# Second layer of an attention and mixture kernel: the polynomial evaluated from PSUM, and the next block's input prepared at other places of the step

## The chip, the cores and the metric

The kernel runs on one core of one Trainium2 chip. A core has five engines that run side by side, each through a queue of its own in program order: TensorE (PE, matrix products into PSUM; its weight loads are listed as PEld), VectorE (DVE), ScalarE (ACT), GpSimd (POOL) and SyncE (SP), which issues the transfers between HBM and SBUF. They wait for each other through semaphores only. The metric is the device time of one execution in microseconds (us).

## The reference

Eight sequences of 576 tokens with eight heads of 64 go through linear attention; the 4608 x 512 result goes through a gated layer (512 to 1536 to 512) and then through the second layer, with which this case is concerned:

```python
def _moe2_ref(x, w_in, w_out, a, b):          # x 4608 x 512, w_in 512 x 2048, w_out 2048 x 512
    h = x @ w_in
    h2 = h * h
    h3 = h2 * h
    P = a[0] + a[1] * h + a[2] * h2 + a[3] * h3
    Q = 1.0 + np.abs(b[0]) * np.abs(h) + np.abs(b[1]) * h2
    g = P / (Q + 1e-06)
    return g @ w_out
...
    x = ...attention of q, k, v...
    x = _moe_ref(x=x, **moe_kwargs)
    return _moe2_ref(x=x, **moe2_kwargs)
```

## The kernel before

All products are made in a reduced 32-bit format of TensorE. To keep the reference's precision every operand x is split into a high part (`th`, `gh`, `wh`: ScalarE copies x into the reduced format) and a low part (`tl`, `gl`: x minus the high part), and a product is three matmuls, high x high, high x low and low x high (`mm3`, L191 to L194). The split of `g` takes its low part on GpSimd (`split`, L183 and L185); that of the second layer's input takes it on VectorE (L1044 and L1046).

The second layer runs from about 966 us to 1787 us of the span. Its 4608 tokens are cut into nine blocks j of 512, the 2048 inner columns into eight groups m of 256: 72 steps i = 8j + m. `h` of a step is a product of 256 rows by 512 columns, built with seven half-size products in the manner of Strassen instead of eight (`product2`, six matmuls of 256 columns each). They accumulate in two PSUM tiles, `px` and `py`, of which there are two pairs, so that a step and the one before it each have one. Between the products, parts of `py` are copied out and added back: ScalarE copies into `s12` and `s5` (L1225, L1230, L1233), VectorE adds `py` (L1236, after product 4) and `px` (L1239, after product 5). Product 6 goes on top of the half of `py` that L1236 has read, so TensorE can begin it only then.

After product n of step i, `close(n)` issues the rest of the work at that place. Each engine's order is the order of issue. `close` calls:

- `vec(i, n)`: the operations on the step before, or on this one, as the table `VEC` lists them for n, each with its lag (1: the step before). For one step they are: ScalarE's square into `r` (L1098), absolute value into `ah` (L1102), and a2 h + a1 into `pp` (L1094), each from PSUM; VectorE's `ah` += b1 r (L1110) and `pp` += a3 r (L1106), which together with a multiplication of `pp` by h in PSUM (L1114, twice, one for `px` and one for `py`) gives P without a0; ScalarE's logarithm of Q into `r` (L1118) and exponential of its negative (L1122), that is 1/Q; two operations of VectorE that refine it (`u1` L1126, `u2` L1130); and `g` = (`pp` + a0) `ah` (L1134). `ah`, `pp` and `r` are tiles of 128 x 1024 in SBUF with two buffers each. `vec_split` splits `g` for the second product.
- the preparation of the next block's input, a generator `building` (`tb_all`): three times a step from m = 1 to 6 one of its pieces is issued, a high part, a low part, or one of GpSimd's four differences `tr` (L1053, L1057, L1060, L1063). The input itself comes into `x_raw`, which has one buffer, by a transfer of 1 MiB issued at the start of step m = 0 (L1202).
- `back_some`: 24 matmuls a step of 512 columns that multiply `g` of three steps earlier by the output weights and sum into four PSUM tiles `accb` (`back_b`, L1150). At a block's end VectorE and ScalarE copy `accb` out (L1156, L1158).
- `pull2`: the transfers of `wi`, the weights of one product, eight products ahead, all from SyncE's queue (L1076).

The tables and the two calls around which the change turns are these:

```python
    VEC = (
        ((vec_g, 2), (on(1, vec_id), 1)), ((on(1, vec_sq), 1), (on(1, vec_abs), 1), (vec_ah, 1), (on(0, vec_split), 2)),
        ((vec_pp, 1), (on(1, vec_split), 2)), ((vec_ln, 1), (on(0, vec_p2), 1)),
        ((vec_exp, 1), ), ((on(1, vec_p2), 1), (vec_u1, 1), (on(0, vec_id), 0)),
        ((vec_u2, 1), (on(0, vec_sq), 0), (on(0, vec_abs), 0)))
...
            if 1 <= m < NM - 1 and n in (1, 3, 5):
                next(building, None)
```

Of the kernel before, what the change touches and what calls it, by code (L numbers as in the profile page):

```python
# [26 lines left out]
HB = NB // 2  # L27
# [109 lines left out]
def kernel(ctx: ExitStack, tc: tile.TileContext, q, k, v, w1, w2, ab_in, out):  # L137
# [16 lines left out]
    def f32(ap):  # L154
        return ap.bitcast(F32)
# [280 lines left out]
    def wfree(n):  # L436
        live[0] -= n
# [596 lines left out]
    def quarter(k, t):  # L1034
        return x_raw[:, 2 * k:2 * k + 2, t * HB:(t + 1) * HB]

    def tb_split(j, n, src, eng):
        if j % 2 == 0 and n > 2:
            h, lo = x_h[:, n - 3, :], x_l[:, n - 3, :]
        else:  # L1040
            h, lo = wnew(F32R, "th"), wnew(F32R, "tl")
        h, lo = (x.rearrange("p (c t) -> p c t", t=HB) for x in (h, lo))
        TB[j, n] = h, lo
        nc.scalar.activation(h, src, AF.Copy)  # L1044
        yield
        eng.tensor_tensor(out=lo, in0=src, in1=f32(h), op=ALU.subtract)  # L1046
        yield

    def tb_all(j):
        b11, b12, b21, b22 = (quarter(k, t) for k in range(2) for t in range(2))  # L1050
        t = wnew(F32, "tr").rearrange("p (c t) -> p c t", t=HB)
        yield from tb_split(j, 0, b11, nc.vector)
        nc.gpsimd.tensor_tensor(out=t, in0=b12, in1=b11, op=ALU.subtract)  # L1053
        yield
        yield from tb_split(j, 1, b21, nc.vector)
        yield from tb_split(j, 3, t, nc.vector)
        nc.gpsimd.tensor_tensor(out=t, in0=b22, in1=t, op=ALU.subtract)  # L1057
        yield
        yield from tb_split(j, 5, b22, nc.vector)
        nc.gpsimd.tensor_tensor(out=b12, in0=b22, in1=b12, op=ALU.subtract)  # L1060
        yield
        yield from tb_split(j, 2, t, nc.vector)
        nc.gpsimd.tensor_tensor(out=t, in0=b21, in1=t, op=ALU.subtract)  # L1063
        yield
        yield from tb_split(j, 4, b12, nc.vector)
        yield from tb_split(j, 6, t, nc.vector)
        wfree(1)

    seq2 = [(i, n) for i in range(NBLK * NM) for n in range(NPROD)]
    ahead2 = [0]  # L1070
# [20 lines left out]

    def vec_id(i, k):
        ps, ah, pp, r = vb[i]
        nc.scalar.activation(pp[:, k], ps[k], AF.Identity, scale=ab[:, 2:3], bias=ab[:, 1:2])  # L1094

    def vec_sq(i, k):
        ps, ah, pp, r = vb[i]
# [3 lines left out]
        ps, ah, pp, r = vb[i]  # L1101
        nc.scalar.activation(ah[:, k], ps[k], AF.Abs, scale=babs[:, 0:1])  # L1102

    def vec_pp(i):
        ps, ah, pp, r = vb[i]
        nc.vector.scalar_tensor_tensor(out=pp, in0=r, scalar=ab[:, 3:4], in1=pp, op0=ALU.mult, op1=ALU.add)  # L1106

    def vec_ah(i):
        ps, ah, pp, r = vb[i]
# [1 line left out]

    def vec_p2(i, k):
        ps, ah, pp, r = vb[i]
        nc.vector.tensor_tensor(out=pp[:, k], in0=pp[:, k], in1=ps[k], op=ALU.mult)  # L1114

    def vec_ln(i):
        ps, ah, pp, r = vb[i]
# [50 lines left out]
    def on(k, fn):  # L1168
        return partial(fn, k=k)

    VEC = (
        ((vec_g, 2), (on(1, vec_id), 1)), ((on(1, vec_sq), 1), (on(1, vec_abs), 1), (vec_ah, 1), (on(0, vec_split), 2)),
        ((vec_pp, 1), (on(1, vec_split), 2)), ((vec_ln, 1), (on(0, vec_p2), 1)),
        ((vec_exp, 1), ), ((on(1, vec_p2), 1), (vec_u1, 1), (on(0, vec_id), 0)),
        ((vec_u2, 1), (on(0, vec_sq), 0), (on(0, vec_abs), 0)))

    def vec(i, n):
        for fn, lag in VEC[n]:
# [19 lines left out]

    for i in range(NBLK * NM):
        j, m = divmod(i, NM)  # L1200
        if m == 0 and j + 1 < NBLK:
            nc.sync.dma_start(out=x_raw, in_=x3_d[j + 1].rearrange("m p c -> p m c"))  # L1202
            building = tb_all(j + 1)
        if i > 2:
            backs += [back_b(i - 3, k) for k in range(2)]
        share = BACK_SHARE if i > 2 else (5, ) * 7
        ps = [ps_w.tile([P, NB], F32, tag=n, name=n) for n in ("px", "py")]
        vec_new(i, ps)
        xl, xr, yl, yr = (x[:, t * HB:(t + 1) * HB] for x in ps for t in range(2))
        s12 = tb.tile([P, NB], F32, tag="s12", name="s12")  # L1210
        s5 = tb.tile([P, HB], F32, tag="s5", name="s5")

        def close(n):
            vec(i, n)
            if 1 <= m < NM - 1 and n in (1, 3, 5):
                next(building, None)
            if m == NM - 2 and n == 6:
                run(building)
            back_some(share[n])
            if n in (1, 3, 5):  # L1220
                fetch_some()
            pull2(i * NPROD + n + 1 + AHEAD)

        product2(i, 0, yl)
        nc.scalar.activation(s12[:, :HB], yl, AF.Copy)  # L1225
        close(0)
        product2(i, 1, xl)
        close(1)
        product2(i, 2, yl)
        nc.scalar.activation(s12[:, HB:], yl, AF.Copy)  # L1230
        close(2)
        product2(i, 3, xr)
        nc.scalar.activation(s5, xr, AF.Copy)  # L1233
        close(3)
        product2(i, 4, yl)
        nc.vector.tensor_tensor(out=yr, in0=yl, in1=s5, op=ALU.add)  # L1236
        close(4)
        product2(i, 5, xr)
        nc.vector.tensor_tensor(out=ps[0], in0=ps[0], in1=s12, op=ALU.add)  # L1239
        close(5)  # L1240
        product2(i, 6, yl)
        close(6)
        if i == 2:
            back_all()
        if m == NM - 1:
            wfree(14 if j % 2 else 6)
# [48 lines left out]
```

## Time and profile before

| what | value |
| --- | --- |
| median of three runs | 1795.63 us (1794.71 to 1796.7) |
| the profiled execution | 1794.12 us, of which the span 1792.0 |
| mean granted clock of TensorE | 0.991 of 2.4 GHz |
| TensorE, matmuls | 1715.8 us busy, 96% of the span |
| TensorE, weight loads | 1444.8 us, 81% |
| VectorE | 1470.3 us, 82% |
| ScalarE | 1130.3 us, 63% |
| GpSimd | 604.5 us, 34% |
| DMA | 348.01 MB, 194 GB/s over the span |

The profiled execution's own time is the span plus what lies around it (2.1 us). Busy shares are of the whole span, in which the attention, the first layer and the second layer follow each other with different loads; what a change to the second layer is worth has to be read within that layer, step by step. The matmuls' ends are modelled, so TensorE's busy time is not a proof that it runs at its peak; where it waits, the row of the waiting matmul says for how long and for whom.

### The profile page before, as it was taken

The numbers are of one execution on the slowest core, as the hardware profiler recorded it, in microseconds if no ns is written. First come the engines' busy times: TensorE is split into PE (matmuls) and PEld (weight loads), VectorE is DVE, ScalarE is ACT, GpSimd is POOL, SyncE is SP. The second block draws the span as 40 slices with busy tenths as digits, with TensorE's granted clock in tenths as the row PEclk, the third lists the DMA queues.
The fourth block names the chain that finished last, engine by engine and source line by source line (L and its number), as shares of the span: only waits on it lengthen the run. The fifth ranks groups of instructions, "written<-read, shape, count | busy, mean of one in ns | idle before, by whom it ended". The sixth has DMA issues, their size and how long they took to land.

```text
span 1792.0 us, 27297 instructions
## 1 busy us (share of the span) xinstructions
PE 1715.8 (96%) x9480; PEld 1444.8 (81%) x9480; DVE 1470.3 (82%) x1914; ACT 1130.3 (63%) x1897; POOL 604.5 (34%) x380
## 2 busy tenths in 40 slices
PE   5989999999999999999999999999999999999998
PEld 4767877888778887788887888888888888888897
DVE  8998897646665657677775899999999999999997
ACT  4565446555664466544444677777777777777775
POOL 2013342211223312252225434343434344434433
PEclk8999999999999999999999999999999999999999
DMA  6551775235674556548986875655565556555550
GB/s 212 175 179 65 246 247 178 63 117 187 224 245 136 199 187 215 194 141 277 329 298 233 310 238 172 230 172 192 172 223 176 189 177 217 171 190 185 184 200 24
DMA packets 193128, 348.01 MB, mean 194 GB/s; under 512 B 18912, under 2 KB 54752, under 8 KB 192992
## 3 DMA queue, kind: packets, MB, share of 16 engines
q1 hardware_dynamic: 192992, 346.27, 57.6%
q8 instruction: 76, 1.25, 0.3%
q14 instruction: 60, 0.49, 0.1%
HBM read 282.23 MB, written 63.96 MB: 193 GB/s over the span
## 4 chain that ended last, share of the span: by engine, by line
PE 63%; DVE 17%; ACT 9%; issue 6%; DMA 3%; POOL 1%; SPq 0%; ACTq 0%; DVEq 0%; POOLq 0%
PE accb L1150 13%; PE acc L477 13%; DVE pp L1106 3%; PE pa L192 3%; PE pa L193 3%; PE pa L194 3%; PE py L192 3%; PE py L193 2%; PE py L194 2%; DMA wi<-wi 2%; PE px L193 2%; PE px L194 2%; PE px L192 2%; DVE tl L1046 2%; ACT pp L1094 2%
## 5 line engine op out<-in xcount | busy, mean ns | idle before, releaser
L185 POOL TENSOR_TENSOR gl<-pp,gh 128x512 fp32r<-128x512 f32 x144 | 275.7, 1935 | 456.0 <-ACT gh L183 299.8
L1150 PE MATMUL accb<-wh,gh 128*128 128x512 f32 x576 | 185.3, 394 | 2.5 <-ACT gh L183 2.2
L1150 PE MATMUL accb<-wl,gh 128*128 128x512 f32 x576 | 185.6, 395 | 0.0
L1150 PE MATMUL accb<-wh,gl 128*128 128x512 f32 x576 | 185.0, 394 | 0.0
L1118 ACT ACTIVATE r<-ah,ln_bias 128x1024 f32<-128x1024 f32 x72 | 82.9, 1151 | 156.3 <-DVE pp L1106 156.3
L1106 DVE SCALAR_TENSOR_TENSOR pp<-r,ab,pp 128x1024 f32<-128x1024 f32 x72 | 165.5, 2299 | 0.0
L192 PE MATMUL py<-th,wi 128*128 128x256 f32 x416 | 118.3, 284 | 14.8 <-DVE py L1236 13.5
L185 POOL TENSOR_TENSOR gl<-ga,gh 128x512 fp32r<-128x512 f32 x36 | 51.3, 1425 | 226.2 <-ACT gh L183 226.0
L194 PE MATMUL py<-tl,wi 128*128 128x256 f32 x416 | 117.3, 282 | 0.0
L193 PE MATMUL py<-th,wi 128*128 128x256 f32 x416 | 117.1, 281 | 0.0
L1150 PEld LDWEIGHTS accb<-wh,gl 128*128 128x128 f32 x576 | 100.2, 189 | 13.4
L1150 PEld LDWEIGHTS accb<-wh,gh 128*128 128x128 f32 x576 | 100.4, 189 | 13.1 <-ACT gh L183 2.7
L1150 PEld LDWEIGHTS accb<-wl,gh 128*128 128x128 f32 x576 | 100.5, 189 | 10.1
L1110 DVE SCALAR_TENSOR_TENSOR ah<-r,babs,ah 128x1024 f32<-128x1024 f32 x72 | 92.5, 1284 | 19.2 <-ACT ah L1102 18.6
L192 PEld LDWEIGHTS py<-th,wi 128*128 128x128 f32 x416 | 78.5, 189 | 30.5 <-DVE py L1236 20.1
L183 ACT ACTIVATE gh<-pp 128x512 fp32r<-128x512 f32 x144 | 92.6, 644 | 13.4 <-DVE pp L1134 12.2
L1126 DVE SCALAR_TENSOR_TENSOR ah<-ah,r 128x1024 f32<-128x1024 f32 x72 | 88.0, 1222 | 12.9 <-ACT r L1122 12.7
L185 POOL TENSOR_TENSOR hl<-val,hl 128x512 fp32r<-128x512 f32 (+1 forms) x32 | 38.2, 1194 | 171.0 <-ACT hl L183 84.2
L1134 DVE SCALAR_TENSOR_TENSOR pp<-pp,ab,ah 128x1024 f32<-128x1024 f32 x72 | 92.4, 1283 | 2.3
L1130 DVE SCALAR_TENSOR_TENSOR ah<-ah,r 128x1024 f32<-128x1024 f32 x72 | 89.0, 1236 | 1.9
L477 PE MATMUL acc<-gh,wh 128*128 128x512 f32 x288 | 88.6, 402 | 0.0
L477 PE MATMUL acc<-gl,wh 128*128 128x512 f32 x288 | 86.1, 394 | 0.4 <-POOL gl L185 0.4
(235 smaller groups left out, 5405.4 us busy)
## 6 DMA issues: line engine op xcount, KB each, us to landing
wi<-wi SPq DMA_DIRECT2D x504, 256.0 KB, 4.7
ws<-ws SPq DMA_DIRECT2D x252, 256.0 KB, 5.0
raw<-in_w SPq DMA_DIRECT2D x68, 512.0 KB, 4.8
v<-in_v SPq DMA_DIRECT2D x30, 325.0 KB, 4.1
k<-in_k SPq DMA_DIRECT2D x30, 320.0 KB, 3.7
q<-in_q SPq DMA_DIRECT2D x36, 256.0 KB, 3.7
x_raw<-x SPq DMA_DIRECT2D x9, 1024.0 KB, 7.7
out<-ob SPq DMA_DIRECT2D x36, 256.0 KB, 2.5
```

Source lines behind the costliest of these rows:

```text
L183: nc.scalar.activation(h, src, AF.Copy)
L185: lo_eng.tensor_tensor(out=lo, in0=src, in1=f32(h), op=ALU.subtract)
L192: nc.tensor.matmul(ps, wh, xh, start=first, stop=False, **kw)
L193: nc.tensor.matmul(ps, wl, xh, start=False, stop=False, **kw)
L194: nc.tensor.matmul(ps, wh, xl, start=False, stop=last, **kw)
L477: nc.tensor.matmul(accs["a", j][m], x[:, m * P:(m + 1) * P], y, start=(f == 0 and n == 0), stop=(f == NF1 - 1 and n == 2))
L1106: nc.vector.scalar_tensor_tensor(out=pp, in0=r, scalar=ab[:, 3:4], in1=pp, op0=ALU.mult, op1=ALU.add)
L1110: nc.vector.scalar_tensor_tensor(out=ah, in0=r, scalar=babs[:, 1:2], in1=ah, op0=ALU.mult, op1=ALU.add)
L1126: nc.vector.scalar_tensor_tensor(out=ah, in0=ah, scalar=q_one, in1=r, op0=ALU.add, op1=ALU.mult)
L1130: nc.vector.scalar_tensor_tensor(out=ah, in0=ah, scalar=2.0, in1=r, op0=ALU.subtract, op1=ALU.mult)
L1134: nc.vector.scalar_tensor_tensor(out=pp, in0=pp, scalar=ab[:, 0:1], in1=ah, op0=ALU.add, op1=ALU.mult)
L1150: nc.tensor.matmul(accs["b", j][t], x[:, t * P:(t + 1) * P], y, start=(f == 0 and n == 0), stop=(f == NF2 - 1 and n == 2))
```

## The change

The polynomial is evaluated in Horner's form. ScalarE's operation from PSUM now makes a3 h + a2 (L1096). `vec_pp`, the VectorE operation on 128 x 1024 with two inputs in SBUF, is gone. In its place the two multiplications by h in PSUM come first (`vec_p1`, L1108, a plain product), and two new operations follow (`vec_p2`, L1116): `pp` = (`pp` + a1) h, with a1 a column of one scalar for each partition, `pp` in SBUF and h in PSUM. VectorE thus has one operation more in a step.

The table `VEC` is written anew. Both of ScalarE's copies into `pp` and VectorE's `ah` and `g` follow product 0; the logarithm and the first multiplication product 1; both splits of `g` and the second multiplication product 2; the exponential and both new operations product 3; `u1` and `u2` stay behind products 5 and 6, and the squares and absolute values of both halves are taken in the same step.

The generator is gone. Of the next block's input, each step from m = 1 issues one high part and at most one of GpSimd's differences after product 4, and from m = 2 one low part right behind `g`, after product 0. The seventh low part of a block is issued in the block's own step m = 0. The transfer into `x_raw` stands behind it, in `close(0)` of step m = 0, and reads or writes nothing else than before. TensorE's instructions keep their order.

```diff
-    def tb_split(j, n, src, eng):
+    def tb_hi(j, n):
...
+    def tb_lo(j, n):
+        h, lo = TB[j, n]
+        nc.vector.tensor_tensor(out=lo, in0=tb_src.pop(n), in1=f32(h), op=ALU.subtract)
...
+    def tb_add(j, n):
+        b11, b12, b21, b22 = (quarter(k, t) for k in range(2) for t in range(2))
+        if n == 3:
+            tb_src["t"] = wnew(F32, "tr").rearrange("p (c t) -> p c t", t=HB)
+        t = tb_src["t"]
+        out, x, y = {3: (t, b12, b11), 2: (t, b22, t), 4: (b12, b22, b12), 6: (t, b21, t)}[n]
+        nc.gpsimd.tensor_tensor(out=out, in0=x, in1=y, op=ALU.subtract)
...
-        nc.scalar.activation(pp[:, k], ps[k], AF.Identity, scale=ab[:, 2:3], bias=ab[:, 1:2])
+        nc.scalar.activation(pp[:, k], ps[k], AF.Identity, scale=ab[:, 3:4], bias=ab[:, 2:3])
...
-    def vec_pp(i):
+    def vec_p1(i, k):
         ps, ah, pp, r = vb[i]
-        nc.vector.scalar_tensor_tensor(out=pp, in0=r, scalar=ab[:, 3:4], in1=pp, op0=ALU.mult, op1=ALU.add)
+        nc.vector.tensor_tensor(out=pp[:, k], in0=pp[:, k], in1=ps[k], op=ALU.mult)
...
     def vec_p2(i, k):
         ps, ah, pp, r = vb[i]
-        nc.vector.tensor_tensor(out=pp[:, k], in0=pp[:, k], in1=ps[k], op=ALU.mult)
+        nc.vector.scalar_tensor_tensor(
+            out=pp[:, k], in0=pp[:, k], scalar=ab[:, 1:2], in1=ps[k], op0=ALU.add, op1=ALU.mult)
...
     VEC = (
-        ((vec_g, 2), (on(1, vec_id), 1)), ((on(1, vec_sq), 1), (on(1, vec_abs), 1), (vec_ah, 1), (on(0, vec_split), 2)),
-        ((vec_pp, 1), (on(1, vec_split), 2)), ((vec_ln, 1), (on(0, vec_p2), 1)),
-        ((vec_exp, 1), ), ((on(1, vec_p2), 1), (vec_u1, 1), (on(0, vec_id), 0)),
-        ((vec_u2, 1), (on(0, vec_sq), 0), (on(0, vec_abs), 0)))
+        ((on(0, vec_id), 1), (on(1, vec_id), 1), (vec_ah, 1), (vec_g, 2)),
+        ((vec_ln, 1), (on(0, vec_p1), 1)),
+        ((on(0, vec_split), 2), (on(1, vec_split), 2), (on(1, vec_p1), 1)),
+        ((vec_exp, 1), (on(0, vec_p2), 1), (on(1, vec_p2), 1)),
+        (),
+        ((vec_u1, 1), (on(0, vec_sq), 0), (on(0, vec_abs), 0)),
+        ((vec_u2, 1), (on(1, vec_sq), 0), (on(1, vec_abs), 0)))
+    TB_LO = (4, None, 0, 3, 1, 2, 5, 6)
+    TB_HI = (None, 0, 3, 1, 2, 5, 6, 4)
+    TB_ADD = (None, 3, 4, 2, None, 6, None, None)
...
-            if 1 <= m < NM - 1 and n in (1, 3, 5):
-                next(building, None)
-            if m == NM - 2 and n == 6:
-                run(building)
+            if n == 0:
+                if m == 0 and 0 < j:
+                    tb_lo(j, 4)
+                if m == 0 and j + 1 < NBLK:
+                    nc.sync.dma_start(out=x_raw, in_=x3_d[j + 1].rearrange("m p c -> p m c"))
+                if 1 < m and j + 1 < NBLK:
+                    tb_lo(j + 1, TB_LO[m])
+            if n == 4 and j + 1 < NBLK:
+                if TB_HI[m] is not None:
+                    tb_hi(j + 1, TB_HI[m])
+                if TB_ADD[m] is not None:
+                    tb_add(j + 1, TB_ADD[m])
```

VectorE, one step in the middle of a block, before, from one addition `py` to the next (`r`, `ab` and `babs` are the square and the columns of coefficients, `tl` the low part of the next block's input):

```order
L1236 TENSOR_TENSOR py<-py,s_13612 128x256
L1239 TENSOR_TENSOR px<-px,s_13611 128x512
L1114 TENSOR_TENSOR pp<-pp,py 128x512
L1126 SCALAR_TENSOR_TENSOR ah<-ah,r 128x1024
L1130 SCALAR_TENSOR_TENSOR ah<-ah,r 128x1024
L1134 SCALAR_TENSOR_TENSOR pp<-pp,ab,ah 128x1024
L1110 SCALAR_TENSOR_TENSOR ah<-r,babs,ah 128x1024
L1046 TENSOR_TENSOR tl<-tr,th 128x512
L1106 SCALAR_TENSOR_TENSOR pp<-r,ab,pp 128x1024
L1114 TENSOR_TENSOR pp<-pp,px 128x512
L1236 TENSOR_TENSOR py<-py,s_13732 128x256
```

The same stretch of VectorE's queue now:

```order
L1250 TENSOR_TENSOR py<-py,s_13645 128x256
L1253 TENSOR_TENSOR px<-px,s_13644 128x512
L1129 SCALAR_TENSOR_TENSOR ah<-ah,r 128x1024
L1133 SCALAR_TENSOR_TENSOR ah<-ah,r 128x1024
L1112 SCALAR_TENSOR_TENSOR ah<-r,babs,ah 128x1024
L1137 SCALAR_TENSOR_TENSOR pp<-pp,ab,ah 128x1024
L1051 TENSOR_TENSOR tl<-tr,th 128x512
L1108 TENSOR_TENSOR pp<-pp,px 128x512
L1108 TENSOR_TENSOR pp<-pp,py 128x512
L1116 SCALAR_TENSOR_TENSOR pp<-pp,ab,px 128x512
L1116 SCALAR_TENSOR_TENSOR pp<-pp,ab,py 128x512
L1250 TENSOR_TENSOR py<-py,s_13765 128x256
```

The multiplication of `py` that stood behind the additions now stands ahead of the next ones; between the low part `tl` and the addition `py` there are four operations that read PSUM, where there were the large `pp` and one; `ah` comes ahead of `g`.

SyncE, around the transfer into `x_raw` at the start of a block, before, with what each issue waits for (the names in brackets are the engines, or the DMA queue's slots, on whose semaphore it waits):

```order
L1076 DMA wi<-wi_144 128x512 [waits DMAHW5_49]
L1076 DMA wi<-wi_145 128x512 [waits DMAHW6_49,DVE_49,Activation_49]
L1202 DMA x_raw<-x_6_158 128x4x512 [waits DMAHW7_49]
L1076 DMA wi<-wi_145 128x512 [waits DMAHW0_49,PE_49]
L1076 DMA wi<-wi_145 128x512 [waits DMAHW1_49,PE_49]
```

And now:

```order
L1078 DMA wi<-wi_144 128x512 [waits DMAHW5_49,PE_49]
L1078 DMA wi<-wi_145 128x512 [waits DMAHW6_49]
L1225 DMA x_raw<-x_6_158 128x4x512 [waits DVE_49,DMAHW7_49,Activation_49,Pool_49]
L1078 DMA wi<-wi_145 128x512 [waits DMAHW0_49,PE_49]
L1078 DMA wi<-wi_145 128x512 [waits DMAHW1_49]
```

The transfer keeps its place in the queue, between the same two transfers of `wi`; it now waits for VectorE, ScalarE and GpSimd, because the seventh low part reads `x_raw` in the same step.

## Rows read from the trace of the kernel before

**Rows 1.** Windows by step: start:end, us, busy (x instructions) PE PEld DVE ACT POOL, PEclk, DMA, GB/s

```profile
1429.08:1439.62 10.54, 10.54 (x67) 9.50 (x66) 10.24 (x11) 8.56 (x16) 5.77 (x3) 1.00 0.42 126
...
1460.77:1472.69 11.92, 10.80 (x67) 9.41 (x66) 11.16 (x11) 8.24 (x15) 5.72 (x3) 1.00 0.77 277
1472.69:1484.61 11.92, 10.80 (x67) 9.41 (x66) 11.15 (x11) 8.24 (x15) 5.72 (x3) 1.00 0.51 155
1484.61:1496.56 11.95, 10.81 (x67) 9.43 (x66) 11.00 (x10) 8.29 (x15) 3.57 (x2) 1.00 0.51 156
```

**Rows 2.** Timeline of TensorE, a long step: start, us, instruction, [wait <-releaser]

```profile
1406.48 0.39 PE L192 MATMUL py<-x_h,wi 128*128 128x256 f32 x1 [1.14 <-DVE py L1236]
```

**Rows 3.** Timeline of VectorE, the same step

```profile
1400.14 1.28 DVE L1110 SCALAR_TENSOR_TENSOR ah<-r,babs,ah 128x1024 f32<-128x1024 f32 x1 [0.45 <-ACT ah L1102]
1401.34 1.78 DVE L1046 TENSOR_TENSOR tl<-x_raw,th 128x512 fp32r<-128x512 f32 x1
1403.05 2.31 DVE L1106 SCALAR_TENSOR_TENSOR pp<-r,ab,pp 128x1024 f32<-128x1024 f32 x1
1405.39 0.69 DVE L1114 TENSOR_TENSOR pp<-pp,px 128x512 f32<-128x512 f32 x1
1406.00 0.43 DVE L1236 TENSOR_TENSOR py<-py,s 128x256 f32<-128x256 f32 x1
```

**Rows 4.** Timeline of GpSimd, the same step: two splits in one row

```profile
1400.76 3.51 POOL L185 TENSOR_TENSOR gl<-pp,gh 128x512 fp32r<-128x512 f32 x2 [6.21 <-PE accb L1150]
```

**Rows 5.** VectorE by line, 1100 to 1792 us: busy us, mean ns | idle before

```profile
L1126 DVE SCALAR_TENSOR_TENSOR ah<-ah,r 128x1024 f32<-128x1024 f32 x62 | 75.8, 1222 | 11.4 <-ACT r L1122 11.3
...
L1156 DVE TENSOR_SCALAR ob<-accb 128x512 f32<-128x512 f32 x16 | 10.9, 681 | 5.8 <-PE accb L1150 5.8
...
L1046 DVE TENSOR_TENSOR x_l<-tr,x_h 128x512 fp32r<-128x512 f32 x8 | 5.5, 682 | 0.0
```

**Rows 6.** Single lines, whole run: least/median/greatest ns, first and last start

```profile
L1106 DVE SCALAR_TENSOR_TENSOR pp<-r,ab,pp x72: 1274/2315/2323, 985.4 to 1772.5; 128x1024 f32<-128x1024 f32 x72
...
L1114 DVE TENSOR_TENSOR pp<-pp,px x72: 686/686/689, 986.7 to 1774.9; 128x512 f32<-128x512 f32 x72
...
L391 DVE SCALAR_TENSOR_TENSOR kvl<-ps_kv,rs,kvh x64: 265/284/293, 12.2 to 719.6; 64x64 fp32r<-64x64 f32 x64
...
L185 POOL TENSOR_TENSOR gl<-pp,gh x144: 1297/1825/2300, 997.5 to 1783.1; 128x512 fp32r<-128x512 f32 x144
```

**Rows 7.** Timeline of ScalarE, the step that begins at 1758.02

```profile
1758.93 0.39 ACT L1225 ACTIVATE s<-py 128x256 f32<-128x256 f32 x1 [0.40 <-PE py L194]
...
1759.87 0.60 ACT L1098 ACTIVATE r<-py 128x512 f32<-128x512 f32 x1
1760.35 0.70 ACT L1102 ACTIVATE ah<-py,babs 128x512 f32<-128x512 f32 x1
```

**Rows 8.** DMA issues in short windows: count, KB each, us from issue to landing

```profile
x_raw<-x SPq DMA_DIRECT2D x1, 1024.0 KB, 6.3
...
x_raw<-x SPq DMA_DIRECT2D x1, 1024.0 KB, 8.2
...
wi<-wi SPq DMA_DIRECT2D x1, 256.0 KB, 8.4
```

**Rows 9.** Timeline of SyncE's issues, ahead of the block that begins at 1418.54

```profile
1410.58 0.43 SPq L1202 DMA_DIRECT2D x_raw<-x  x1
1411.10 3.04 SPq L1076 DMA_DIRECT2D wi<-wi  x5
```

**Rows 10.** Timeline of TensorE and ScalarE behind the last product

```profile
1781.86 0.50 PE L1150 MATMUL accb<-wh,gh 128*128 128x512 f32 x1 [2.24 <-ACT gh L183]
...
1774.96 1.15 ACT L1118 ACTIVATE r<-ah,ln_bias 128x1024 f32<-128x1024 f32 x1 [2.34 <-DVE pp L1106]
```

**Rows 11.** Waits, 966 to 1066 us: waiting <- awaited: us in all, count, longest

```profile
PE py L192 <- DVE py L1236: 4.6, 4, 1.2
...
PE py L192 <- ACT s L1225: 0.8, 1, 0.8
```

More of the change, by code (lines that the diff above doesn't have):

```diff
@@ L1035, in quarter @@
         return x_raw[:, 2 * k:2 * k + 2, t * HB:(t + 1) * HB]
-    def tb_split(j, n, src, eng):
+    tb_src = {}
+    def tb_hi(j, n):
         if j % 2 == 0 and n > 2:
@@ L1041, in tb_split @@
             h, lo = wnew(F32R, "th"), wnew(F32R, "tl")
-        h, lo = (x.rearrange("p (c t) -> p c t", t=HB) for x in (h, lo))
-        TB[j, n] = h, lo
+        TB[j, n] = h, lo = tuple(x.rearrange("p (c t) -> p c t", t=HB) for x in (h, lo))
+        src = {0: quarter(0, 0), 1: quarter(1, 0), 5: quarter(1, 1), 4: quarter(0, 1)}.get(n, tb_src.get("t"))
+        tb_src[n] = src
         nc.scalar.activation(h, src, AF.Copy)
-        yield
-        eng.tensor_tensor(out=lo, in0=src, in1=f32(h), op=ALU.subtract)
@@ L1047, in tb_split @@
-        yield
-    def tb_all(j):
[L1050 to L1067, printed above, removed]
+    def tb_lo(j, n):
+        h, lo = TB[j, n]
+        nc.vector.tensor_tensor(out=lo, in0=tb_src.pop(n), in1=f32(h), op=ALU.subtract)
+        if n == 6:
+            tb_src.pop("t")
+            wfree(1)
@@ new lines, in tb_add @@
+    def tb_add(j, n):
[5 more added lines that the diff above has]
+        nc.gpsimd.tensor_tensor(out=out, in0=x, in1=y, op=ALU.subtract)
+    def tb_all(j):
+        for fn, n in ((tb_hi, 0), (tb_add, 3), (tb_lo, 0), (tb_hi, 1), (tb_lo, 1), (tb_hi, 3), (tb_lo, 3), (tb_add, 2),
+                      (tb_hi, 2), (tb_add, 4), (tb_lo, 2), (tb_add, 6), (tb_hi, 5), (tb_lo, 5), (tb_hi, 4), (tb_lo, 4),
+                      (tb_hi, 6), (tb_lo, 6)):
+            fn(j, n)
+            yield
@@ L1200 @@
         j, m = divmod(i, NM)
-        if m == 0 and j + 1 < NBLK:
-            nc.sync.dma_start(out=x_raw, in_=x3_d[j + 1].rearrange("m p c -> p m c"))
-            building = tb_all(j + 1)
         if i > 2:
```

## The prediction, made before the changed kernel ran

> **What bounds the kernel now.** I read the layer in question step by step first. One step of the second layer is 42 matmuls of 256 columns (seven products of six) and 24 of 512 (the products of three steps earlier with the output weights, "backs" below). Cut into steps [rows 1], a block shows two kinds: five steps of about 10.54 us in which TensorE is busy from end to end, and three (m = 4, 5, 6) of 11.92, 11.92 and 11.95. The clock column reads 1.00 in both, the upper level, so the clock is not the difference. A block has 4.2 us (1.38 + 1.38 + 1.41) that TensorE spends on nothing. The mean step is 10.54 + 4.2/8 = 11.07.
>
> Next, who holds TensorE in the long steps: product 6 waits 1.14 us for VectorE's addition `py` (L1236) [rows 2]. And why `py` is late: VectorE's queue just ahead of it [rows 3] holds a split of the next block's input (1.78 us) and the combination `pp` (2.31). Both are two-input operations on SBUF, and both lie beside GpSimd's two splits [rows 4]; undisturbed, the same split takes 0.68 [rows 5] and `pp` 1.27 [rows 6]. They lose 1.1 and 1.04 us, one GpSimd operation (1.30 at least [rows 6]) less what had already run. The Trainium skill (SBUF — State Buffer, section "SBUF: two separate sides") states it as a lock: a VectorE instruction with two SBUF inputs and a GpSimd one exclude each other for the whole instruction; the 1.78 and 2.31 agree.
>
> Then what is not held: VectorE's multiplication of `pp` by PSUM has 0.686, 0.686 and 0.689 us as least, median and greatest of 72 [rows 6], though it often lies beside GpSimd. So one SBUF and one PSUM input escape. VectorE is busy 10.24 us in a plain step and 11.16 in a long one [rows 1]: in the long steps it is the bound, in the others TensorE.
>
> **The change part by part.** TensorE's order of instructions is unchanged, and so is the number of ScalarE's and GpSimd's in a step.
>
> *Polynomial.* Out goes `pp` on 1024 columns, 2.31 us as it runs [rows 6]; the two multiplications by PSUM stay in kind (0.69 each), and two operations with a scalar column, one SBUF and one PSUM input come in. The trace has no such operation at 128x512. Below: nothing cheaper than the 0.69 of the plain multiplication. Above: the scalar column costs 0.06 at 1024 columns (1.28 [rows 3] against the 1.22 of an operation whose scalar is a constant [rows 5]), so 0.75. I take 0.69; the ends differ by 0.12 a step, inside idle time. VectorE's step then is `ah` and `g` 1.20 each (start to start [rows 3]; one begins 0.08 before the other ends), `u1` and `u2` 1.24 each (no overlap, each needs the one before), `px` and the plain two 0.61 each (1405.39 to 1406.00 [rows 3]), the new two 0.67 at most, `py` 0.35: 8.4, with a split 9.0, against 10.54 of TensorE.
>
> *The order on one queue.* Idle time is not enough; the additions must come in time. Count from the start S of a step's first product. A step of 42 + 2 x 24 units makes a product 0.70 and a back 0.234. The previous `py` is final at S - 0.70, ScalarE sees it 0.21 later (the copy at 1758.93 in the step that began at 1758.02, after a product of 0.70 [rows 7]), then square 0.48 to the next start and absolute value 0.70 [rows 7]: S + 0.7. VectorE still has `u2` until S + 1.0. From there `ah` 1.0, `g` 2.2, split 3.4, two multiplications done by 4.7, two of the new form by 6.0, or 6.6 with their waits on one another. `py` needs product 4, seen at 6.76, and is done at 7.2; TensorE wants it for product 6 at 9.13: 1.9 us to spare where it now misses by 1.14. `px` follows at 8.4, `u1` 9.0, `u2` 10.25 to 11.5, which is S + 1.0 of the next step, as assumed. So the loop closes below TensorE's period.
>
> *GpSimd.* `g` is done at 3.5, ScalarE reaches the high parts after its logarithm and a copy, about 4.15, and GpSimd's splits run from 4.8 to 6.1 and 7.4, a sum to 8.7: all of it beside PSUM operations, and before `u1`. Margin 0.3; if a sum slips into `u1`, VectorE loses up to 1.30 in that step of its 1.5 idle. Price 0, at most a fraction.
>
> *Steps m = 2 and 3* also carry two evacuations of output (0.68 each [rows 5]) between `u1`, `u2` and `ah`. Everything there comes 1.2 later, which leaves 0.7 of the 1.9. I take 0; were it 0.5 a block, 3.5 us in all.
>
> *The load of the next input* moves. It used to wait for nothing in the step; now it waits for the split of product 4's input, done at S + 4.1, and SyncE's whole queue waits behind it, the weights of the next step first. Now the first goes out at S + 4.7 and is wanted by product 1 of the next step at 10.54 + 0.70 + 0.70 = S + 11.95. The trace has no such load behind an empty queue: of the eight here two landed 6.3 and 8.2 us after issue, with loads ahead of them [rows 8]; the weights issued 0.52 behind one land at 8.4, so 0.7 after it [rows 8, 9]. From S + 4.2 that is S + 11.2 or S + 13.1: 0.75 early or 1.15 late. I take the early end, because a queue whose issuer is waiting has drained. The Trainium skill (SBUF — State Buffer, section "The DMA setup-cost knee") gives about 2 us and the bytes at 436 GB/s, an estimate of 4.4 us for 1 MiB, by which nothing would wait; no run here shows such a load alone.
>
> *End and start.* Behind the last product the logarithm waits 2.34 us for `pp`, which still reads the tile it overwrites; the last backs start 2.24 us late [rows 10]. Without `pp` the last high part comes 2.34 sooner, at 1779.5, and TensorE's wait begins at 1779.6 (1781.86 less 2.24): all 2.2 us go. In block 0 four waits of the same kind hold 4.6 us [rows 11], with a refill of 0.2 each 5.5. The 0.8 for a copy at the layer's start [rows 11] hangs on the first block's splits, which are reordered too; I leave it in and let the low end take it out.
>
> **Sum.** Seven blocks x 4.2 = 29.4; block 0 5.5; end 2.2: 37.1 us. The profiled execution took 1794.1 (span 1792.0), the median of the runs is 1795.6, 1.5 above it. 1794.1 - 37.1 = 1757.0, and as a median 1758.5; I say 1758.
>
> **Rivals.**
> A, the forecast: TensorE bound in all steps, 1754 to 1762.
> B, the weights come late behind the moved load: 1.15 in each of seven blocks, 8 us: 1766. For it: the 8.2 row, and that the load waits where it did not. Against: the drained queue.
> C, the new operation is held by GpSimd after all. Its second reading from SBUF is only a scalar per partition, and the one row of that kind, a small one (64x64, PSUM, scalar, SBUF), lies between 0.265 and 0.293 us 64 times [rows 6], never one GpSimd operation longer. The Trainium skill (VectorE: DVE Perf Modes, section "Two Vector instructions with no wait between them") counts a pointer scalar among the SBUF inputs that the compiler compares; if the lock counted so too, this rival would hold. Price: each of the two waits out about 0.85 of a split, and in half the steps 1.30 of a sum on top: 9.0 + 1.7 + 0.6 = 11.3 less what the idle ends swallow, about the present 11.07: 1795, no change.
> D, the slower side: every VectorE operation that touches SBUF takes turns with GpSimd, the PSUM ones too. Then a step is VectorE's 9.1 (outputs included) and GpSimd's 2.5 operations of 1.30 in a row, 12.35, against 11.07 over 69 steps: 88 us more, 1882. It is slower than now from 2.0 us of holding a step (11.07 - 9.1). Against it stand the 72 equal times of the multiplication.
> E, the change does not do what it says: GpSimd's work slides out from under the PSUM operations, into `u1` or the next `ah`. With 1.5 us idle that costs 0 to 1 us in each of the four steps a block with a sum: at the middle 0.5 x 4 x 8 = 16 us, 1774, at worst 1790.
>
> **How the numbers follow.** A 0.64, B 0.13, C 0.10, D 0.06, E 0.07. C is about even, two of its ten faster and three slower. Faster: 0.64 + 0.13 + 0.07 + 0.02 = 0.86; within 0.2% 0.05; slower 0.03 + 0.06 = 0.09. About 0.2% (3.6 us) is what a measurement of this kernel can tell from no change. The range takes A and B, with the 0.8 and two small waits of block 0 gone and a run's spread below (1754), and above the 3.5 us of the output steps on B (1770) and the middle of E (1774); C, D and the upper half of E stay out, 0.2 in all.
>
> **What the changed profile would show.** Right: steps of 10.54 at m = 4 to 6; no wait of TensorE for `py`; the new operations at 0.69 to 0.75, the splits on GpSimd near 1.3 instead of 1.94, `tl` near 0.68. B: TensorE waiting for a `wi` load in product 1 of m = 1. C: the new form near 1.5 beside GpSimd. D: the plain multiplication longer than 0.69 too. E: `u1` or `ah` above 2 us. What would make it wrong altogether: a wait on ScalarE that I priced at nothing, since the copies that free `py` and `px` now stand behind the logarithm, with 1.6 us to spare by the schedule above.

## The result and the profile after

| | before | after |
| --- | --- | --- |
| median | 1795.17 us (1792.87 to 1796.7) | 1755.58 us (1755.21 to 1756.32) |
| ratio | | 0.9781, 95% interval 0.9764 to 0.9798 |
| span of the profiled execution | 1792.0 us | 1753.4 us |

The change makes the kernel 2.2% faster. 1758 us was forecast, 1754 to 1774 as the range.

The page of after begins with the busy times. Columns: busy us, share of the span, instructions.

```profile
span 1753.4 us, 27298 instructions
...
PE 1707.2 (97%) x9480; PEld 1447.5 (83%) x9480; DVE 1361.4 (78%) x1986; ACT 1132.0 (65%) x1897; POOL 490.0 (28%) x380
```

VectorE has 72 instructions more (one a step) and 109 us less busy time, GpSimd the same instructions and 114 us less. GpSimd's 114 us are time in which VectorE held it. VectorE's 109 are what is left of its own held time after some 15 us of added work: 144 operations of 0.743 us came and 72 of 1.27 (undisturbed) went. Cut into steps, in the columns of [rows 1] (these are m = 3, 4 and 5):

```profile
1427.14:1437.68 10.54, 10.54 (x68) 9.50 (x67) 9.97 (x14) 8.64 (x16) 3.82 (x3) 1.00 0.85 286
1437.68:1448.22 10.54, 10.54 (x68) 9.50 (x67) 9.01 (x12) 8.38 (x15) 2.56 (x2) 1.00 0.73 243
1448.22:1458.76 10.54, 10.54 (x68) 9.50 (x67) 9.00 (x12) 8.37 (x15) 3.81 (x3) 1.00 0.59 174
```

Steps of 11.92 are gone: m = 4 and 5 take 10.54 like all other steps of blocks 1 to 8, TensorE is busy from end to end, and VectorE has 9.0 us of work in them. TensorE's waits in the layer were led before by the 25 for `py`, four in block 0 and three in each of the next seven (waiting <- awaited: us in all, count, longest):

```profile
PE py L192 <- DVE py L1236: 28.3, 25, 1.2
```

Now a single wait is left, in block 0, for a copy of the first layer's output. It took 0.3 us before:

```profile
PE accb L1153 <- ACT xo L488: 0.8, 1, 0.8
```

VectorE in the step that begins at 1437.68 (timeline, the columns of [rows 3]):

```profile
1438.56 1.29 DVE L1112 SCALAR_TENSOR_TENSOR ah<-r,babs,ah 128x1024 f32<-128x1024 f32 x1
...
1440.95 0.69 DVE L1051 TENSOR_TENSOR tl<-x_raw,th 128x512 fp32r<-128x512 f32 x1
1441.56 0.69 DVE L1108 TENSOR_TENSOR pp<-pp,px 128x512 f32<-128x512 f32 x1
...
1442.75 0.75 DVE L1116 SCALAR_TENSOR_TENSOR pp<-pp,ab,px 128x512 f32<-128x512 f32 x1
1443.41 0.75 DVE L1116 SCALAR_TENSOR_TENSOR pp<-pp,ab,py 128x512 f32<-128x512 f32 x1
1444.52 0.43 DVE L1250 TENSOR_TENSOR py<-py,s 128x256 f32<-128x256 f32 x1 [0.36 <-ACT r L1125]
1446.08 0.70 DVE L1253 TENSOR_TENSOR px<-px,s 128x512 f32<-128x512 f32 x1 [1.14 <-PE px L194]
```

and GpSimd beside it:

```profile
1442.43 2.56 POOL L185 TENSOR_TENSOR gl<-pp,gh 128x512 fp32r<-128x512 f32 x2 [6.21 <-issue]
```

Two splits take 2.56 us where [rows 4] had 3.51, and they lie beside four operations that read PSUM. `tl` takes 0.69 instead of 1.78. `py` is done at 1444.95, which is S + 7.27 (S is the start of the step's first product), and VectorE idles 0.36 and 1.14 us, 1.5 in the step. The new operation and GpSimd's split over the whole run (least/median/greatest ns), beside [rows 6]:

```profile
L1116 DVE SCALAR_TENSOR_TENSOR pp<-pp,ab,px x72: 736/743/747, 983.6 to 1737.3; 128x512 f32<-128x512 f32 x72
...
L185 POOL TENSOR_TENSOR gl<-pp,gh x144: 1291/1301/1318, 999.1 to 1745.1; 128x512 fp32r<-128x512 f32 x144
```

Neither is ever held: the new form spreads over 11 ns, the split over 27, where the split had 1297 to 2300.

### The profile page after: what moved, and what is told of

It is laid out like the page before. It is cut to its first block, busy times and chain, and to the rows that moved or that the text cites. A ratio compares the mean times of both kernels' runs of the same rounds, so it can differ in the third digit from the quotient of the medians.

```text
span 1753.4 us, 27298 instructions
## 1 busy us (share of the span) xinstructions
PE 1707.2 (97%) x9480; PEld 1447.5 (83%) x9480; DVE 1361.4 (78%) x1986; ACT 1132.0 (65%) x1897; POOL 490.0 (28%) x380
## 4 chain that ended last, share of the span: by engine, by line
PE 82%; DVE 9%; issue 4%; ACT 2%; DMA 2%; POOL 1%; SPq 0%; ACTq 0%; DVEq 0%; POOLq 0%
PE accb L1153 23%; PE acc L477 14%; PE py L193 4%; PE py L194 4%; PE py L192 4%; PE pa L192 3%; PE px L193 3%; PE pa L194 3%; PE pa L193 3%; PE px L194 3%; PE px L192 3%; PE pc L192 2%; PE pc L193 2%; PE pc L194 2%; PE pg L192 1%
## 5 line engine op out<-in xcount | busy, mean ns | idle before, releaser
L185 POOL TENSOR_TENSOR gl<-pp,gh 128x512 fp32r<-128x512 f32 x144 | 184.1, 1301 | 528.7 <-ACT gh L183 314.4
L1100 ACT ACTIVATE r<-px 128x512 f32<-128x512 f32 x72 | 43.1, 599 | 135.9 <-DVE px L1253 135.9
L1253 DVE TENSOR_TENSOR px<-px,s 128x512 f32<-128x512 f32 x72 | 50.4, 700 | 77.4 <-PE px L194 77.4
L1133 DVE SCALAR_TENSOR_TENSOR ah<-ah,r 128x1024 f32<-128x1024 f32 x72 | 88.1, 1223 | 2.1
L477 PE MATMUL acc<-gh,wl 128*128 128x512 f32 x288 | 86.1, 394 | 0.0
```

Of the source, the lines that this page charges most:

```text
L185: lo_eng.tensor_tensor(out=lo, in0=src, in1=f32(h), op=ALU.subtract)
L477: nc.tensor.matmul(accs["a", j][m], x[:, m * P:(m + 1) * P], y, start=(f == 0 and n == 0), stop=(f == NF1 - 1 and n == 2))
L1100: nc.scalar.activation(r[:, k], ps[k], AF.Square)
L1133: nc.vector.scalar_tensor_tensor(out=ah, in0=ah, scalar=2.0, in1=r, op0=ALU.subtract, op1=ALU.mult)
```

## The experiments

The leading theory is that of the prediction: a VectorE operation with two inputs in SBUF and a GpSimd operation take turns, one with an input in PSUM escapes, and the gain is the held time that leaves the stretch ahead of `py`. The change does this in three ways at once (polynomial, order of the vector work, place of the input preparation), so the first question is which of them is needed.

| kernel | median us | ratio to before, 95% interval |
| --- | --- | --- |
| after | 1755.58 | 0.9764 to 0.9798 |
| poly_alone | 1755.97 | 0.9772 to 0.9801 |
| input_alone | 1758.41 | 0.9770 to 0.9812 |
| order_alone | 1767.36 | 0.9835 to 0.9864 |
| sbuf_operand | 1799.59 | 1.0013 to 1.0034 |
| splits_late | 1759.79 | 0.9788 to 0.9826 |
| load_late | 1763.58 | 0.9816 to 0.9849 |
| two_more | 1756.06 | 0.9772 to 0.9802 |
| three_more | 1781.41 | 0.9912 to 0.9941 |
| poly_two_more | 1790.56 | 0.9972 to 0.9991 |
| constant_a1 | 1753.39, one run | |

### The polynomial alone

To the kernel before, with `vec_id` and `vec_p2` as in the change:

```diff
-    def vec_pp(i):
+    def vec_p1(i, k):
...
-        nc.vector.scalar_tensor_tensor(out=pp, in0=r, scalar=ab[:, 3:4], in1=pp, op0=ALU.mult, op1=ALU.add)
+        nc.vector.tensor_tensor(out=pp[:, k], in0=pp[:, k], in1=ps[k], op=ALU.mult)
...
-        ((vec_pp, 1), (on(1, vec_split), 2)), ((vec_ln, 1), (on(0, vec_p2), 1)),
+        ((on(0, vec_p1), 1), (on(1, vec_p1), 1), (on(1, vec_split), 2)), ((vec_ln, 1), (on(0, vec_p2), 1)),
```

> The order of before, with the polynomial alone exchanged: in the place of the large pp (two inputs in SBUF, 2.31 us) the two multiplications by PSUM, and behind them the two operations with the column. Theory (VectorE operations with two SBUF inputs wait out GpSimd's, those with one PSUM input do not): ahead of py the queue is shorter by 2.34 - 2 x 0.61 = 1.1 us, less 0.06 for the column, against a wait of 1.14 in the three long steps, so 0.1 us or nothing is left in each: 1756 to 1763 us; the split tl still takes 1.78 beside GpSimd. Rival (the gain comes from where the operations stand, not from which they are): the long steps stay near 11.9 and the time near 1793.

Measured: 1755.97 us, the time of the whole change. A step m = 5 reads, in the columns of [rows 1]:

```profile
1449.31:1459.85 10.54, 10.54 (x68) 9.50 (x66) 10.17 (x12) 8.41 (x15) 4.75 (x3) 1.00 0.61 176
```

and one group of VectorE's input splits, by line (busy us, mean ns | idle before):

```profile
L1046 DVE TENSOR_TENSOR x_l<-x_raw,x_h 128x512 fp32r<-128x512 f32 x8 | 14.3, 1785 | 0.0
```

The split is still held as before (1785 ns in the mean of this group, 1.78 us in the step shown), and the step is TensorE's all the same: 10.17 us of VectorE fit into 10.54. The 0.1 us of waiting that the theory allowed for is not there. In this step `py` begins at S + 7.83, in the step m = 5 of before at S + 9.94. Of these 2.1 us, 1.1 are the exchanged operations; the other 1.0 is gained ahead of them, since VectorE reaches `ah` at S + 3.07 instead of S + 4.09. So the exchange of one operation carries the time, and the rival is out for this half. What the other parts of the change add is small: by the starts of the steps 1.3 us, all in block 0 (92.6 us here, 91.3 in after).

### The input preparation alone

To the kernel after: polynomial and `VEC` of before put back, so that only `tb_hi`, `tb_lo`, `tb_add`, their places and the load differ from before.

> The polynomial and the order of the vector work of before; only the preparation of the next block's input is that of after (low part right behind g, high part and GpSimd's sums behind product 4, the load behind the seventh low part). Theory (what counts is that one of the two held operations leaves the stretch ahead of py): tl takes 0.68 instead of 1.78 and fills the 0.45 that VectorE waits there anyway, pp stays at 2.3; py comes at least 1.3 us earlier, so the 1.14 of waiting are gone: 1757 to 1765, the 2.2 at the end remain. Rival (pp beside GpSimd is what holds py): long steps stay, 1785 or above. Second rival: the sums now beside u1 cost what is gained, 1770 to 1785.

Measured: 1758.41 us. VectorE in a step of m = 5 (timeline):

```profile
1453.64 0.68 DVE L1051 TENSOR_TENSOR tl<-tr,th 128x512 fp32r<-128x512 f32 x1
1454.24 1.28 DVE L1112 SCALAR_TENSOR_TENSOR ah<-r,babs,ah 128x1024 f32<-128x1024 f32 x1
1455.44 2.31 DVE L1108 SCALAR_TENSOR_TENSOR pp<-r,ab,pp 128x1024 f32<-128x1024 f32 x1
```

Here `pp` is held in 71 of 72 steps (2.30 us or more) and TensorE waits for nothing between 1100 and 1745 us. `tl` now stands ahead of `ah`, where nothing holds it (0.68) and where VectorE waited before. From the start of `g` to that of `py` it is 5.95 us in this step, against 7.58 in the step m = 5 of before, and these 1.6 us are more than the 1.14 that were missing. What is left beside after is the wait at the end, which this kernel keeps:

```profile
PE accb L1152 <- ACT gh L183: 2.2, 1, 2.2
```

So either of the two held operations may stay; the two together were too much.

### The order of the vector work, with the old polynomial

To the kernel after: `vec_pp` put back with the plain multiplication by PSUM, in this place:

```diff
-        ((on(0, vec_id), 1), (on(1, vec_id), 1), (vec_ah, 1), (vec_g, 2)),
-        ((vec_ln, 1), (on(0, vec_p1), 1)),
-        ((on(0, vec_split), 2), (on(1, vec_split), 2), (on(1, vec_p1), 1)),
+        ((on(0, vec_id), 1), (on(1, vec_id), 1), (vec_ah, 1), (vec_pp, 1), (vec_g, 2)),
+        ((vec_ln, 1), ),
+        ((on(0, vec_split), 2), (on(1, vec_split), 2)),
```

> The order and the input preparation of after, with the polynomial of before (pp on 128x1024 between ah and g, so that it stands ahead of GpSimd's splits). Theory: pp takes 1.27 undisturbed instead of 2.31, VectorE has about the same 9.0 us of work a step, py starts near S + 7.0 against 9.13 wanted; the logarithm waits for pp, 1.2 us later, which ScalarE has idle. Then nearly the whole gain comes from the order too: 1756 to 1765, the 2.2 us at the end not regained. Rival (the polynomial from PSUM is what matters): long steps of 11.5 or more, 1785 or above. Second rival: ScalarE's copy s12 behind the late logarithm holds product 4: steps of 10.7 to 11.2, 1770 to 1800.

Measured: 1767.36 us, 2 above the first theory's range, and the second rival has its share. `pp` is not held (1283 ns in the mean), but the logarithm waits for it, and with it ScalarE's queue. ScalarE in a step m = 3, and TensorE's waits over 960 to 1810 us:

```profile
1438.49 1.15 ACT L1120 ACTIVATE r<-ah,ln_bias 128x1024 f32<-128x1024 f32 x1 [2.30 <-DVE pp L1108]
1439.55 0.36 ACT L1243 ACTIVATE s<-py 128x256 f32<-128x256 f32 x1
...
PE py L192 <- ACT s L1243: 5.3, 8, 0.7
PE px L192 <- DMA wi<-wi: 1.8, 7, 0.5
```

Eight times the copy `s12` behind the late logarithm keeps TensorE from product 4, and seven times the weights behind the moved load are late; the low part that the load waits for stands behind `pp` here. These waits are 7.1 us, 1.2 more stand at the end, and the steps in which they fall grow by more than the waits: by the starts of the steps in blocks 1 to 7, the steps m = 1 (weights) are 3.6 us longer in all than in after and the steps m = 3 (`s12`) 6.6. With block 0 (0.9) and the end (1.4) this accounts for the 12 us above after. `u1` has 1505 ns in the mean against 1227 in after, so GpSimd's later work holds it at times: in the steps m = 2 and m = 5 it takes 1984 and 1947 ns, and both steps stay at 10.54. But behind m = 2 come the two copies of output on VectorE, and there the held `u1` makes `ah`, `pp` and so the logarithm of m = 3 late (VectorE's timeline, ahead of the step above):

```profile
1431.73 2.01 DVE L1128 SCALAR_TENSOR_TENSOR ah<-ah,r 128x1024 f32<-128x1024 f32 x1
...
1435.39 0.68 DVE L1158 TENSOR_SCALAR ob<-accb 128x512 f32<-128x512 f32 x1
...
1437.19 1.27 DVE L1108 SCALAR_TENSOR_TENSOR pp<-r,ab,pp 128x1024 f32<-128x1024 f32 x1
```

### The same operations with an operand in SBUF

To the kernel after; the polynomial becomes another one, the times are what counts:

```diff
-        nc.vector.tensor_tensor(out=pp[:, k], in0=pp[:, k], in1=ps[k], op=ALU.mult)
+        nc.vector.tensor_tensor(out=pp[:, k], in0=pp[:, k], in1=ah[:, k], op=ALU.mult)
...
-            out=pp[:, k], in0=pp[:, k], scalar=ab[:, 1:2], in1=ps[k], op0=ALU.add, op1=ALU.mult)
+            out=pp[:, k], in0=pp[:, k], scalar=ab[:, 1:2], in1=ah[:, k], op0=ALU.add, op1=ALU.mult)
```

> The kernel after, but the four operations p1 and p2 read the tile ah in SBUF where they read h in PSUM (so the polynomial is another one); order, counts and sizes are the same. Theory: now all four exclude GpSimd's two splits, which lie in the same 2.5 us (2.56 us): the step gets 2.56 us longer on VectorE less its 1.5 idle, up to 1.06 a step over 69 steps: 1790 to 1830, and some of the four operations above 1.3 us. Rival (the place of the operand does not matter): 1755, all four at 0.62 to 0.75.

Measured: 1799.59 us, 44 above after, and the whole gain is gone though order, sizes and counts are those of after. VectorE and GpSimd in a step m = 4 (timelines), a window of the step behind it (m = 5), and TensorE's waits over 960 to 1810 us:

```profile
1470.29 1.28 DVE L1108 TENSOR_TENSOR pp<-pp,ah 128x512 f32<-128x512 f32 x2
1471.49 3.49 DVE L1116 SCALAR_TENSOR_TENSOR pp<-pp,ab,ah 128x512 f32<-128x512 f32 x2
...
1470.68 3.75 POOL L185 TENSOR_TENSOR gl<-pp,gh 128x512 fp32r<-128x512 f32 x2 [5.65 <-issue]
...
1476.89:1488.92 12.03, 10.78 (x67) 9.38 (x66) 12.00 (x12) 8.13 (x15) 4.75 (x3) 1.00 0.48 153
...
PE py L192 <- DVE py L1250: 26.7, 44, 1.4
```

Two operations of 0.75 take 3.49 us, the two splits of GpSimd 3.75 instead of 2.56, VectorE is the bound at 12.00 of 12.03, and TensorE waits for `py` again. That the operand lies in PSUM is what makes the new form free.

### Room on VectorE: two and three operations more

To the kernel after, behind the new operations and ahead of `py`, into a tile that nobody reads (three times for the second kernel):

```diff
+        for _ in range(2):
+            nc.vector.tensor_tensor(out=spare, in0=pp[:, 0], in1=ps[0], op=ALU.mult)
```

> The kernel after, with two more plain multiplications by PSUM a step on VectorE (128x512, into a spare tile that nobody reads), ahead of the addition py. Theory: VectorE has 9.0 us of work in a step of 10.54, and the additions have 1.9 us to spare; 2 x 0.61 = 1.2 more fits into both. Only the two steps a block with output on VectorE can miss by some tenths: 1755 to 1760. Rival (VectorE has no such room, its idle time is taken by waits that move with it): 1.2 a step show up, up to 1830.

> The same with three: 1.85 more, 10.9 of work in 10.54 us. Theory: VectorE becomes the bound by 0.3 us a step and a little more in the steps with output: 4 to 5 us a block, 1785 to 1800, TensorE waiting for py. Rival (the additions' 1.9 us to spare is what counts, not the sum): 1756 to 1760.

Measured: 1756.06 and 1781.41 us. A step of each, m = 7 with two and m = 5 with three:

```profile
1469.50:1480.04 10.54, 10.54 (x68) 9.50 (x67) 10.20 (x14) 8.36 (x15) 2.56 (x2) 1.00 0.38 125
```

```profile
1464.92:1475.81 10.89, 10.81 (x67) 9.41 (x66) 10.79 (x15) 8.15 (x15) 3.80 (x3) 1.00 0.56 169
```

With two the median is that of after, though the layer itself is 2.6 us longer (the step m = 3, which copies output, grows from 10.54 to 10.75) and begins 1.3 us earlier in the profiled execution. The third turns VectorE into the bound: 10.89 a step. The 26 us are less than the 30 to 45 expected: the step m = 1, which has no input split, still takes 10.54 and m = 2 behind it 10.63. So the 1.5 us of idle time are real room. With two the first theory holds; with three it has the bound right and the time 4 us too long.

### The same two in the order of before

To poly_alone, the same two operations behind the first `vec_p2`, ahead of `py`.

> The kernel poly_alone (order of before, new polynomial) with the same two more multiplications, ahead of py. Theory (what the new order buys is room on VectorE, which the time does not show): with some 4 us a block of splits held by GpSimd the block has 87 us of VectorE's work in 84.3: 1775 to 1800, against 1755 to 1760 for the same two in the order of after. Rival (the order buys nothing at all): the same time as two_more.

Measured: 1790.56 us against 1756.06 for two_more. A step m = 5:

```profile
1471.32:1483.03 11.71, 10.80 (x67) 9.42 (x66) 11.43 (x14) 8.29 (x15) 4.74 (x3) 1.00 0.52 158
```

The rest of the change, the order of the vector work and the places of the input preparation together, does buy something: about 1 us of room on VectorE in such a step (10.17 of work in poly_alone, 9.0 in after), which the time of after does not show because TensorE bounds the step at 10.54 either way.

### GpSimd's splits beside operations that it holds

To the kernel after:

```diff
-        ((on(0, vec_split), 2), (on(1, vec_split), 2), (on(1, vec_p1), 1)),
+        ((on(1, vec_p1), 1), ),
...
-        ((vec_u1, 1), (on(0, vec_sq), 0), (on(0, vec_abs), 0)),
+        ((on(0, vec_split), 2), (on(1, vec_split), 2), (vec_u1, 1), (on(0, vec_sq), 0), (on(0, vec_abs), 0)),
```

> The kernel after, with both splits of g moved from behind product 2 to behind product 5, so that GpSimd works beside u1 and u2, which have two inputs in SBUF, instead of beside the operations that read PSUM. Theory: u1 and u2 together lose 1.3 to 2.6 a step, of which 1.5 is idle time; the steps with a sum lose 1.3 more: 1760 to 1800, u1 or u2 above 2 us. Rival (where GpSimd works does not matter now): 1755 to 1757.

Measured: 1759.79 us (1757.38 to 1762.8), 4 above after and just below the theory's range. The four executions lie in two pairs, 1757.4 and 1758.0, 1761.6 and 1762.8; the trace is of the fastest, and what the slower pair lost is not shown. By line, 1100 to 1745 us:

```profile
L1133 DVE SCALAR_TENSOR_TENSOR ah<-ah,r 128x1024 f32<-128x1024 f32 x62 | 125.4, 2023 | 1.9
L1129 DVE SCALAR_TENSOR_TENSOR ah<-ah,r 128x1024 f32<-128x1024 f32 x61 | 90.8, 1488 | 0.0
```

`u2` is held by 0.80 us in the mean and `u1` by 0.26 (1223 and 1227 in after), and the 1.5 idle swallow this nearly everywhere: in blocks 1 to 7 only the step m = 3 grows clearly, to 10.72 to 10.80, and the seven blocks are 1.75 us longer in all. The holding is there, most of its price is not.

### The load of the next input, later

To the kernel after, in the first step of each block but the first: the four operations p1 and p2 are issued ahead of the load instead of at their own places, which leaves VectorE's order as it is, and a small write behind them holds the load:

```diff
                     tb_lo(j, 4)
+                    for fn, lag in late:
+                        fn(i - lag)
+                    nc.vector.memset(x_raw[:, 0, 0:8], 0.0)
```

> The kernel after, but in a block's first step the load into x_raw waits 2.6 us longer: the four operations p1 and p2 of that step are issued ahead of it (they keep their place on VectorE), and a write of 8 columns into x_raw behind them holds it. Nothing else moves. In the kernel after the first weights behind that load land 1.4 to 1.7 us before their product. Theory (the load's wait was free by these 1.4 to 1.7 and by nothing else): the weights come 0.9 to 1.3 late in each of seven blocks, 1762 to 1765, with TensorE waiting for wi. Rival (the load is shortened when it starts later, or the wait is hidden anyway): 1755 to 1757.

Measured: 1763.58 us. In after the block of 1479.84 issues the load and the first weights behind it so (SyncE's timeline, start and us), and those weights land 6.9 us later (KB, us from issue to landing):

```profile
1483.94 0.37 SPq L1225 DMA_DIRECT2D x_raw<-x  x1
1484.41 0.46 SPq L1078 DMA_DIRECT2D wi<-wi  x1
...
wi<-wi SPq DMA_DIRECT2D x1, 256.0 KB, 6.9
```

That is at 1491.3, and product 1 of the next step begins at 1491.78: 0.5 us early, the least of seven blocks; in the other six the same weights are 1.4 to 1.7 early. In load_late the block of 1485.33 issues its load at S + 6.64 instead of S + 4.10, and TensorE waits:

```profile
1491.97 0.37 SPq L1234 DMA_DIRECT2D x_raw<-x  x1
...
PE px L192 <- DMA wi<-wi: 7.1, 7, 2.1
```

Seven waits, one a block: 0.5 to 1.0 us in six, and 2.1 in one, where the weights landed 7.1 us after their issue instead of 5.5 to 6.0. The steps in which they fall are 10.4 us longer in all than in after. The layer begins 3.0 us earlier in this execution (963.97 instead of 966.96), so that 7.5 are left between the two spans. So the load's wait costs nothing in after, by a margin of 0.5 to 1.7 us and by nothing else. A load 2.5 us later is rival B.

### A constant instead of the column

To the kernel after, `scalar=0.25` for `scalar=ab[:, 1:2]`: a1 is another number then.

> The kernel after with a constant in place of the column a1 in the new operation (so the polynomial has another a1). Theory: the column costs 0.06 at 512 columns, the operation takes 0.68 instead of 0.74, and the time stays at 1755, since VectorE has 1.5 idle a step. Rival (the step depends on VectorE's sum): 0.12 a step less, 1747.

Measured, over the whole run:

```profile
L1116 DVE SCALAR_TENSOR_TENSOR pp<-pp,px x72: 673/683/690, 981.3 to 1735.0; 128x512 f32<-128x512 f32 x72
```

0.683 us instead of 0.743: the column costs 0.06. The one run has 1753.39 us, 2.2 below after's median, but the steps are 10.54 as in after and the layer begins at 964.71 instead of 966.96, so this difference lies ahead of the layer and not in the operation.

## Why the prediction was right

*Bound and mechanism.* Held operations made `py` late, TensorE waited 1.14 us for it in three steps of eight, and with the holding gone all steps of blocks 1 to 8 are 10.54. Both are seen in the rows of before and after, and sbuf_operand brings the waits back by the place of an operand alone.

*The sum.* Forecast were 37.1 us; the spans differ by 38.7. By places, from the starts of the steps:

| term | forecast | measured |
| --- | --- | --- |
| blocks 1 to 7 | 29.4 | 29.7 (619.96 to 590.24) |
| block 0 | 5.5 | 6.6 (97.87 to 91.28) |
| last step and its backs | 2.2 | 2.25 (29.57 to 27.32) |
| ahead of the layer and behind it | 0 | 0.1 (0.55 later, 0.67 shorter) |

Only block 0 was mis-sized, in two terms that partly cancel. Its four steps with a wait for `py` lost 5.2 us, not 5.5: the first of them, at 1005 us, is only 1.0 shorter (12.63 to 11.63), because the wait for the copy of the first layer's output grew there from 0.3 to 0.8 us. And two small waits ahead of them, the 0.8 for the copy at the layer's start, which I left in, and one of 0.5 at 1005 us, went as well, 0.75 and 0.64 in their steps. The working put these into the low end, and the time lies between it and the forecast. The 0.1 outside the layer is chance: in after, load_late and constant_a1, which differ in nothing ahead of the layer, it begins at 966.96, 963.97 and 964.71 us.

*The schedule on VectorE.* `py` was to be done at S + 7.2 and is done at S + 7.27; `u1` at S + 9.0 begins at 1446.69, S + 9.01; GpSimd's splits were to begin at S + 4.8 and begin at S + 4.75; work 9.0 in 10.54 was forecast and is read. The one risk named, a wait on ScalarE behind the logarithm, did not come true: its copy `s12` ends at S + 4.10, 1.75 us ahead of product 4, where 1.6 were reckoned. In order_alone, where the logarithm is late, this is the wait that costs most.

*The price of the new form.* I took 0.69, the lower end; it is 0.743, the upper end (0.75). The row of 1.28 against 1.22 had said so, and constant_a1 confirms its 0.06. It cost nothing because of the idle time, as the working says.

*B* was weighed at 0.75 us early or 1.15 late. It is 0.5 to 1.7 early, because the load behind the drained queue lands 5.5 to 6.8 us after its issue, not 6.3 to 8.2. *C* priced a held new form at 1795; sbuf_operand, where it and the plain multiplication can both be held, gives 1799.6. *D* is excluded: the plain multiplication has 682 ns in the median beside GpSimd. *E* was over-priced: I let a held `u1` cost up to 1 us in the steps with a sum, 16 us at the middle, but splits_late, where `u1` and `u2` together are held by 1.06 us a step in the mean, costs 4 us by its median and 1.75 in seven blocks of its trace. The step that fails there is the cost of up to 1 us above the idle time, when one held operation (1.30 at most) is less than the 1.5 idle. In these traces the cost shows only at m = 3, where output copies take that idle time.

*What the prediction did not see.* It added up the parts as if the change were needed as a whole. The three long steps lacked 1.14 us each; in their step m = 5 the polynomial alone brings `py` 2.1 us forward from the step's start, and the other place of the input preparation alone takes 1.6 out of the stretch from `g` to `py`. Either closes the gap, so half of what was done has next to no time in it. The working had the numbers for most of this and did not compare them one by one.

## What to carry to other kernels

Count what a wait is short of before counting what a change takes away: whatever goes beyond it is room, not time, and it shows only once more work is put on that engine. If two engines take turns on SBUF, an exchange for a form with an input in PSUM takes the held time out with the operation: here 2.31 us went, 1.04 of them held, and two operations of 0.74 came that nothing holds. When a queue is put into a new order, ask what now stands behind an operation that waits (here, behind the logarithm, a copy that TensorE needs).

## What the runs showed of the hardware

The Trainium skill (SBUF — State Buffer, section "SBUF: two separate sides") says that a VectorE instruction with two SBUF inputs and a GpSimd instruction that reads SBUF exclude each other for the whole instruction. The rows agree, with a measured pair: the same form at 128x512 with the same scalar column takes 736 to 749 ns of 144 with its second tensor in PSUM, and 735/1779/1865 (least/median/greatest) with it in SBUF, beside the same GpSimd splits:

```profile
L1116 DVE SCALAR_TENSOR_TENSOR pp<-pp,ab,ah x144: 735/1779/1865, 983.6 to 1781.6; 128x512 f32<-128x512 f32 x144
```

What the prediction had left open as its C is settled: the column of scalars, which lies in SBUF too, does not count as a second input (11 ns of spread beside GpSimd). These turns are not taken by semaphores, by which alone the engines wait for each other according to the section on the cores: a held operation has no wait in its row, only a longer time (2.31 us instead of 1.27). And where several operations in a row can be held, the burden falls unevenly: in sbuf_operand the first two of the four have a median of 684 ns and the second two 1779, in splits_late `u1` 1312 and `u2` 2203. So a long row does not by itself tell which operation stands in the wrong place; its neighbours have to be read with it.
